# Strided rows loaded as two halves with a gap between them

## The chip, the cores and the metric

The kernel runs on one core of one Trainium2 chip. The metric is the device time of one execution in microseconds (us): lower is better. Before the change, four runs gave a median of 444.38 us (443.89 to 444.83).

## What is computed

Inputs are `q`, `k`, `v` of shape (8, 8, 576, 64) in float32 (batch, heads, positions, head width) and the weights `moe_w_r`, `moe_w_i` (64 modes of 512x512) and `moe_w_ch` (512x512). Half of the heads use a local mask, the other half a strided one:

```
mask_local   = (rel >= 0) & (rel < 32)
mask_strided = (rel >= 0) & (pos[None, :] % 32 == pos[:, None] % 32)
attn = softmax(where(mask, q @ k.T / 8, -1e9)) @ v        # per batch element and head
x    = attn, heads side by side                            # (8, 576, 512)
X    = rfft(x, axis=1)[:, :64]                             # 64 modes
Y    = X times (w_r[m] + i w_i[m]) per mode                # a 512x512 complex matrix each
u    = x + irfft(Y)
out  = u + relu(u @ w_ch)
```

Heads 4 to 7 are the strided ones: a query at position s sees the keys at s, s-32, s-64 and so on. The weights of the 64 modes are 64 x 512 x 512 x 2 float32 numbers, by far the largest part of what is read.

## The kernel before, in words

All large loads are issued by GpSimd (POOL) on one queue, because they convert float32 in memory to float16 on the chip as they are moved. The queue has eight completion semaphores, used in turn: POOL issues a load only when the load eight places before it has landed. Beyond that, a load waits for its target buffer to be free, and since POOL issues in order, everything behind it waits too.

There are three kinds of loads on this queue:

- Strided `q`, `k`, `v` (24 loads, `load(i)` for i below 8, line 200): the four strided heads of one batch element. The 576 positions of a head are 18 blocks (c) of 32 positions (r). One row of a load is one (head, block), so there are 4 x 18 = 72 rows, on 72 partitions. A row is 32 positions x 64 numbers: 8 KB in memory, 4 KB on the chip.
- Local `q`, `k`, `v` (24 loads, line 205): the four local heads, cut into 128 rows of 18 positions x 64 numbers (4.6 KB in memory, 2.3 KB on the chip).
- Weights (254 loads, `w_fetch`, line 180): half of one mode's matrix, 64 rows of 8 KB in memory, 4 KB on the chip. Each mode takes two loads (real and imaginary part on either half of the partitions), once for the first half of the channels and once for the second; mode 0 has no imaginary part. One load of `w_ch` (line 188, 512 packets) is the only other one.

The tile `qn` (pool `pin`, three buffers) holds the three loads of one `load(i)`: `qn[:, 0]` is q, `qn[:, 1]` is k, `qn[:, 2]` is v, each with 2048 columns. v is loaded first, then q, then k.

The work runs in four stages:

1. Strided attention, b = 0 to 7. For each b TensorE transposes the columns of `qn`, 128 at a time (two positions of all 72 rows), into PSUM: `str_q` (line 237, 16 transposes), and `str_turn` for k and v (line 253, 16 each). VectorE and ScalarE copy the results out; then come masks and scores (lines 313 and 321), exponentials (line 328), values (line 342), normalising (lines 217 and 218) and a small Fourier transform `dft` (line 482). The transposes for b+1 stand between the steps of b. At the start of step b POOL gets `load(b + 3)` and a few weight loads: 18 weight buffers are filled in this stage without waiting for one to be used.
2. Local attention, b = 0 to 7, with the modes of the first half between its steps (line 515, 16 matmuls each). From here on each mode that is done frees a weight buffer and has the next fetched.
3. The modes of the second half, with the output's projections between them.
4. Inverse transform, relu, sums and stores.

`load(8)` (the local rows of b = 0) is issued at step b = 5 of stage 1; its first user is the local transpose of line 363.

Of the kernel before, what the change touches and what calls it, by code (L numbers as in the profile page):

```python
# [11 lines left out]
F16 = mybir.dt.float16  # L12
# [65 lines left out]
def kernel(  # L78
# [27 lines left out]
    def psum(kind, half=False):  # L106
        if half:
            return pss[kind].tile([128, 1024], F16, tag=kind, name=kind)
        return pss[kind].tile([128, 512], FP, tag=kind, name=kind)
# [37 lines left out]
    pin = actx.enter_context(tc.tile_pool(name="pin", bufs=3))  # L147
# [41 lines left out]
        w_chs["n"] = w_ch  # L189


    qns = {}

    def load(i):
        if i >= 2 * B:
            return
        qn = pin.tile([128, 3, 2048], F16, tag="qn", name="qn")
        for vi, src in ((2, v), (0, q), (1, k)):
            if i < B:
                nc.gpsimd.dma_start(  # L200
                    qn[0:72, vi, :],
                    src[i, 4:8].rearrange("h (c r) d -> (h c) (r d)", r=32),
                )
            else:
                nc.gpsimd.dma_start(
                    qn[:, vi, 0:1152],
                    src[i - B, 0:4].rearrange("h (cb i) d -> (h cb) (i d)", i=18),
                )
        qns[i] = qn
# [23 lines left out]
    def str_q(b, g):  # L233
        qn, qT = qns[b], qTs[b % 2]
        tp = psum("tp", half=True)
        for i in range(8):
            nc.tensor.transpose(
                tp[:, ds(72 * i, 72)],
                qn[0:72, 0, ds(128 * (8 * g + i), 128)],
                idn[0:72, 0:72],  # L240
            )
        nc.vector.tensor_copy(
            out=qT.rearrange("p (h r c) -> p r h c", h=4, r=16)[:, ds(8 * g, 8)],
            in_=tp[:, 0:576].rearrange("p (r h c) -> p r h c", h=4, c=NCB),
        )

    def str_turn(b, vi, j):
        qn = qns[b]
        a, z = JG[j]
        nr = z - a  # L250
        tp = psum("tp", half=True)
        for i in range(nr):
            nc.tensor.transpose(  # L253
                tp[:, ds(72 * i, 72)],
                qn[0:72, vi, ds(128 * (a + i), 128)],
                idn[0:72, 0:72],
            )

        def move(eng, dst, pr):
            eng(  # L260
                out=dst[:, ds(72 * a, 72 * nr)].rearrange(
                    "p (h c r) -> p h c r", h=4, r=nr
                ),
                in_=tp[pr, 0 : 72 * nr].rearrange("p (r h c) -> p h c r", h=4, c=NCB),
            )

        if vi == 2:
            move(act_copy if j else nc.vector.tensor_copy, vT[:, 0:1152], ds(0, 128))
            return
        for rp in range(2):  # L270
            pr = ds(64 * rp, 64)
            move(
                act_copy if j == 1 else nc.vector.tensor_copy,
                kzs[b % 2][pr, rp, 0:1152],
                pr,
            )

    def str_k(b, j):
        str_turn(b, 1, j)

    def str_v(b, j):
        str_turn(b, 2, j)
# [392 lines left out]

    psum_pools(tp=3, sc=3, av=2)
    load(0)
    const_load(nc.scalar, "cI", "cM6", "cM5", "cFs")
    load(1)
    const_load(nc.sync, "cMl", "cFl", "cA")  # L680
    load(2)
    w_fetch(2)

    def str_front(b):
        return [
            lambda: str_v(b, 0), lambda: str_v(b, 1),
            lambda: str_v(b, 2), lambda: str_q(b, 0),
            lambda: str_back(b, 0),
            lambda: str_back(b, 1), lambda: str_q(b, 1),
            lambda: str_k(b, 0),  # L690
            lambda: str_k(b, 1), lambda: str_k(b, 2),
        ]
# [271 lines left out]
```

The softmax here doesn't subtract the row's maximum and nothing guards it: scores larger than these inputs give would overflow.

## Time and profile before

| what | value |
|---|---|
| median of four runs | 444.38 us |
| the profiled execution | 444.58 us |
| its span in the trace | 442.7 us |
| stage 1 in the trace | about 6 to 82 us |
| POOL's queue of loads | 26608 packets, 81.28 MB as written on the chip |
| read from memory | 163.37 MB |
| TensorE busy | 339.0 us (77%) |
| VectorE, ScalarE busy | 215.7 us (49%), 188.4 us (43%) |
| one issue of a strided load on POOL | 0.53 us |
| issue to landing, strided loads, median | 11.0 us |

The profiled execution's time is 1.9 us above its span: launch and end lie outside. In the page, the span is cut into 40 slices of 11.07 us; a digit is the busy share in tenths. The chain of waits follows the work that ended last back to the start; a piece "DMA qn<-in_q_dram" in it means that the next step waited for this load to land, counted from its issue. The share of the DMA engines in a stretch can be above 1, because the packets that the trace records for one engine overlap a little.

The trace also has a record of every packet: its queue, start, duration and bytes as written. In the steady stage (250 to 360 us) an 8 KB weight row is recorded with 324 ns, and on one engine the next row starts 305 ns after it. The landing of a load is recorded as 16 increments of its semaphore.

### The profile page before, as it was taken

Reading aid. Unit: us, or ns where it says so; the run is one execution under the profiler, and the core shown is the slowest. Engines: PE = TensorE matmul, PEld = TensorE weight load, DVE = VectorE, ACT = ScalarE, POOL = GpSimd, SP = SyncE. Lnnn points to the kernel's source line nnn. Section 1 sums busy time; section 2 is a strip of 40 time slices with the busy share of each in tenths; the row PEclk is TensorE's granted clock in tenths of the full one; section 3 lists DMA queues with packets and bytes.
Section 4 is the critical chain, followed back from the end, with each engine's and each line's share of the span. In section 5 each row is a group of like instructions: output and inputs, shape, how many; then the busy total and the mean of one; then the engine's idle time right before and its main releaser. Section 6 shows DMA issues by size and latency. Waiting matters only on the chain.

```text
span 442.7 us, 12290 instructions
## 1 busy us (share of the span) xinstructions
PE 339.0 (77%) x5284; PEld 242.3 (55%) x5284; DVE 215.7 (49%) x462; ACT 188.4 (43%) x353; POOL 180.6 (41%) x327
## 2 busy tenths in 40 slices
PE   3887789769999886776775458688686849988994
PEld 2766677648777675564653245455444535654441
DVE  3687868744535434151511024345344542763895
ACT  2586667553545554343441302114222402443882
POOL 5243333422544433443443434444444344420883
PEclk9998989675958988675985558588878767998998
DMA  8999999999999999999999999999999999991687
GB/s 186 181 203 201 200 198 203 208 212 206 172 211 212 212 212 211 214 210 213 211 212 212 210 212 213 213 211 211 213 207 211 212 212 212 212 208 30 262 321 273
DMA packets 30902, 92.35 MB, mean 209 GB/s; under 512 B 5952, under 2 KB 6848, under 8 KB 30848
## 3 DMA queue, kind: packets, MB, share of 16 engines
q0 software_dynamic: 26608, 81.28, 93.9%
q1 hardware_dynamic: 3440, 9.50, 5.7%
q8 instruction: 42, 0.69, 0.6%
q10 hardware_dynamic: 800, 0.77, 0.6%
q14 instruction: 12, 0.10, 0.1%
HBM read 163.37 MB, written 9.44 MB: 390 GB/s over the span
## 4 chain that ended last, share of the span: by engine, by line
DMA 65%; PE 25%; DVE 3%; issue 3%; ACT 1%; POOL 1%; DVEq 0%; POOLq 0%; ACTq 0%
DMA wt<-in_moe_w_i_dram 38%; DMA wt<-in_moe_w_r_dram 11%; DMA qn<-in_q_dram 8%; DMA qn<-in_k_dram 5%; PE y L515 4%; PE tp L363 2%; DMA qn<-in_v_dram 2%; PE sc L613 2%; PE v L860 2%; PE v L648 2%; PE u L663 2%; PE sc L409 2%; PE sc L425 1%; PE sc L482 1%; PE y L482 1%
## 5 line engine op out<-in xcount | busy, mean ns | idle before, releaser
L515 PE MATMUL y<-X,wt 128*128 128x16 f16 (+1 forms) x2048 | 82.6, 192 | 62.5 <-DMA wt<-in_moe_w_i_dram 59.6
L180 POOL DMA_DIRECT2D wt<-in_moe_w_r_dram x128 | 66.2, 517 | 133.8 <-DMA wt<-in_moe_w_r_dram 32.4
L515 PEld LDWEIGHTS <-wt 128*128 128x128 f16 (+1 forms) x2048 | 72.1, 103 | 76.0 <-issue 56.2
L180 POOL DMA_DIRECT2D wt<-in_moe_w_i_dram x126 | 65.1, 517 | 61.0 <-DMA wt<-in_moe_w_i_dram 37.6
L622 ACT ACTIVATE v<-sc 128x512 f16<-128x512 f32 x32 | 19.0, 597 | 88.6 <-PE sc L613 88.4
L613 PE MATMUL sc<-w_cp,xT 128*128 128x512 f16 (+1 forms) x160 | 51.2, 449 | 0.5 <-DVE xT L585 0.4
L439 ACT ACTIVATE PL<-sc 128x480 f16<-128x480 f32 (+1 forms) x48 | 27.4, 579 | 37.8 <-PE sc L425 37.4
L623 DVE COPY xo<-tp 128x512 f16<-128x512 f16 x32 | 22.1, 691 | 39.6 <-PE tp L621 39.6
L218 DVE TENSOR_TENSOR xb<-av,rec 90x256 f16<-90x256 f32 (+2 forms) x80 | 36.0, 450 | 2.8
L217 DVE RECIPROCAL rec<-av 90x4 f32<-90x4 f32 (+2 forms) x80 | 14.7, 183 | 46.5 <-PE av L454 32.6
L370 DVE COPY qT<-tp 128x576 f16<-128x576 f16 x16 | 12.0, 758 | 41.1 <-PE tp L363 36.5
L228 ACT ACTIVATE v<-tp 128x640 f16<-128x640 f16 (+1 forms) x24 | 19.4, 808 | 28.0 <-PE tp L397 24.4
L363 PE MATMUL tp<-cI_s,qn 64*64 64x64 f16 x864 | 26.0, 210 | 3.3 <-DMA qn<-in_q_dram 1.8
L328 ACT ACTIVATE PS<-sc 90x360 f16<-90x360 f32 (+1 forms) x48 | 22.8, 489 | 10.3 <-PE sc L321 9.9
L873 POOL TENSOR_TENSOR rl<-rl,xo 128x512 f32<-128x512 f32 x16 | 18.3, 1155 | 18.9 <-ACT rl L871 18.5
L890 DVE TENSOR_TENSOR osb<-u,rl 128x512 f32<-128x512 f32 x36 | 23.8, 689 | 2.7 <-ACT rl L871 1.3
L363 PEld LDWEIGHTS <-qn 64*64 64x64 f16 x864 | 20.4, 122 | 8.2 <-issue 3.0
L482 PEld LDWEIGHTS <-xb 108*128 108x128 f16 (+2 forms) x176 | 18.1, 119 | 12.0 <-DVE xb L218 6.2
L565 DVE COPY xT<-tp 128x512 f16<-128x512 f16 x16 | 11.0, 689 | 25.2 <-DMA wt<-in_moe_w_i_dram 15.6
L409 PE MATMUL sc<-cMl_s,cI_s 128*128 128x480 f16 (+1 forms) x48 | 21.6, 451 | 1.6 <-ACT X L228 1.6
L613 PEld LDWEIGHTS <-xT 128*128 128x128 f16 (+1 forms) x160 | 14.8, 110 | 14.6 <-issue 6.6
L253 PE MATMUL tp<-cI_s,qn 72*128 72x72 f16 x256 | 14.8, 207 | 10.0 <-DMA qn<-in_v_dram 7.2
(94 smaller groups left out, 654.5 us busy)
## 6 DMA issues: line engine op xcount, KB each, us to landing
wt<-in_moe_w_r_dram POOLq DMA_DIRECT2D x128, 256.0 KB, 9.4
wt<-in_moe_w_i_dram POOLq DMA_DIRECT2D x126, 256.0 KB, 9.6
out_dram<-osb SPq DMA_DIRECT2D x14, 512.0 KB, 2.7
qn<-in_v_dram POOLq DMA_DIRECT2D x16, 288.0 KB, 10.5
qn<-in_q_dram POOLq DMA_DIRECT2D x16, 288.0 KB, 10.7
qn<-in_k_dram POOLq DMA_DIRECT2D x16, 288.0 KB, 11.1
out_dram<-osb SPq DMA_DIRECT2D x7, 128.0 KB, 2.4
out_dram<-osb SPq DMA_DIRECT2D x3, 256.0 KB, 2.8
```

Of the source, the lines that this page charges most:

```text
L180: nc.gpsimd.dma_start(wt[ds(64 * ri, 64)], src[m, ds(256 * half, 256), :].rearrange("(p c) e -> p c e", c=4),)
L218: nc.vector.tensor_tensor(out=dst, in0=val.rearrange("p h (q c) -> p h c q", c=4), in1=rec[0:n, 0:pieces] .to_broadcast((n, pieces, 64)) . ...
L228: nc.scalar.activation(out=out, in_=in_, func=ACTF.Copy)
L328: nc.scalar.activation(out=PS[0:n, ds(POFF[t], 4 * n)], in_=scp[0:n, 0 : 4 * n], func=ACTF.Exp, scale=SCALE,)
L363: nc.tensor.transpose(tp[ds(64 * hp, 64), ds(64 * i, 64)], qn[ds(64 * hp, 64), vi, ds(64 * (9 * g + i), 64)], idn[ds(64 * hp, 64), ds(64 * ...
L409: nc.tensor.matmul(scp[:, 0 : n * times].rearrange("p (h x) -> p h x", h=times), idn, mask_rows("cMl", n, times), start=True, stop=False,)
L439: nc.scalar.activation(out=dst, in_=src, func=ACTF.Exp, scale=SCALE)
L482: nc.tensor.matmul(xp[:, ds(192 * cp, 192)], xb[b][0:n, base + t, ds(128 * cp, 128)], F[0:n, t, :], start=(i == 0), stop=(i == len(tiles) ...
L515: nc.tensor.matmul(yv[:, mi, e, :], wt[pr, XC[c], ds(128 * e, 128)], Xh[half][pr, c, :, :, m], start=(c == 0), stop=(c == 3),)
L613: nc.tensor.matmul(vp[pr, :], xT[:, ch, cols], w_chs["cp"][:, ch, :], start=(ch == 0), stop=(ch == 3),)
L623: nc.vector.tensor_copy(out=xo[pr].rearrange("p (h q c) -> p h q c", h=2, c=4), in_=tp[pr, 0:512].rearrange("p (h c q) -> p h q c", h=2, c=4),
L890: nc.vector.tensor_tensor(out=osb[:, t % 2, :], in0=up, in1=rls[b, t][:, t % 2, :], op=AluOp.add)
```

## The change

Each of q, k and v in `qn` gets 2 x 1040 columns instead of 2048: the first half of a row (positions r = 0 to 15 of the block) goes to columns 0 to 1023, the second half (r = 16 to 31) to columns 1040 to 2063, with 16 unused columns behind each half. The target of a strided load is thereby no longer one run of 4 KB per row but two runs of 2 KB, which cannot be merged. The source is the same run of memory, described as 144 runs of 4 KB. The transposes take their 128 columns from the new places (`pair_cols`). The local loads still fill 1152 columns from column 0 of each third, which now starts at multiples of 2080 columns. The order of all instructions on all engines is the same as before.

```
+    HALF = 1024 + 16
     qns = {}
+
+    def pair_cols(i):
+        return ds(HALF * (i // 8) + 128 * (i % 8), 128)
...
-        qn = pin.tile([128, 3, 2048], F16, tag="qn", name="qn")
+        qn = pin.tile([128, 3, 2 * HALF], F16, tag="qn", name="qn")
         for vi, src in ((2, v), (0, q), (1, k)):
             if i < B:
                 nc.gpsimd.dma_start(
-                    qn[0:72, vi, :],
-                    src[i, 4:8].rearrange("h (c r) d -> (h c) (r d)", r=32),
+                    qn[0:72, vi, :].rearrange("p (f x) -> p f x", f=2)[:, :, 0:1024],
+                    src[i, 4:8].rearrange("h (c f r) d -> (h c) f (r d)", f=2, r=16),
                 )
...
-                qn[0:72, 0, ds(128 * (8 * g + i), 128)],
+                qn[0:72, 0, pair_cols(8 * g + i)],
...
-                qn[0:72, vi, ds(128 * (a + i), 128)],
+                qn[0:72, vi, pair_cols(a + i)],
```

## The prediction, made before the result was known

> **What bounds the kernel now.** I read the page's slices first, then the DMA queues, the chain of waits, the issues on POOL's queue and last TensorE's waits. From the page:
>
> ```profile
> span 442.7 us, 12290 instructions
> ...
> DMA  8999999999999999999999999999999999991687
> GB/s 186 181 203 201 200 198 203 208 212 206 172 211 212 212 212 211 214 210 213 211 212 212 210 212 213 213 211 211 213 207 211 212 212 212 212 208 30 262 321 273
> ...
> q0 software_dynamic: 26608, 81.28, 93.9%
> ...
> DMA 65%; PE 25%; DVE 3%; issue 3%; ACT 1%; POOL 1%; DVEq 0%; POOLq 0%; ACTq 0%
> ```
>
> The DMA engines are full until the last tenth, and the chain is 65% DMA. From slice 11 on, where only weights and local rows are loaded, the rate stays at 210 to 214 GB/s; in slices 2 to 6, where the strided rows are loaded, it is 198 to 203, equally full by the digits. The packet count tells why. The known packets of POOL's queue are 254 x 64 weight rows, 24 x 128 local rows, 24 x 72 strided rows, 512 for w_ch and 16 completion writes for each of 303 loads: 26416. The 192 left are 8 per strided load, and 72 + 8 = 80 = 16 x 5: the 72 rows are dealt five to an engine and filled up. So 14 engines move five rows, one two, one none. The landings say the same: of the 16 increments of the first v load two come at 4.02 and 4.99 us, the other fourteen between 5.62 and 6.33; of the load at 63.88 us two come at 65.48 and 66.79, fourteen between 72.96 and 74.97. A load is as late as its busiest engine, and the engines' queues are never empty.
>
> The chain of waits in 0 to 100 us:
>
> ```profile
> 5.03 14.49 DMA qn<-in_q_dram
> 19.52 0.28 issue
> 19.80 11.64 DMA wt<-in_moe_w_r_dram
> 31.44 0.28 issue
> 31.73 11.39 DMA qn<-in_k_dram
> 43.11 0.28 issue
> 43.40 10.53 DMA qn<-in_q_dram
> ...
> 71.36 10.66 DMA qn<-in_q_dram
> 82.02 0.04 issue
> 82.07 1.17 PE tp L363 x19
> ```
>
> Each piece is one turn of the eight semaphores: a load lands, the load eight later is issued. The local stage starts at 82.07 because the first local q landed at 82.02; all 24 strided loads are ahead of it on the queue. From 82 to 148 us the chain runs through TensorE, and from 148.6 to 373 through weight loads, eight per 9.91 us (1.239 us each). The stream of weights is full again from about 121 us; a delay or gain at 82 us goes through to the end. How much TensorE waited in stage 1 (timeline of TensorE; in brackets idle before):
>
> ```profile
> 52.35 0.53 PE L253 MATMUL tp<-cI_s,qn 72*128 72x72 f16 x11 [0.82 <-DMA qn<-in_v_dram]
> 53.98 0.62 PE L237 MATMUL tp<-cI_s,qn 72*128 72x72 f16 x8 [0.43 <-DMA qn<-in_q_dram]
> ```
>
> After the first load it waits for no rows until 52.35 us, then 0.8, 0.4, 0.5 (q near 64), 0.3 (q near 73) and 1.8 us (before 82.07): 3.8 in all. So the loads are only just the slower side: TensorE can use up to 3.8 us.
>
> **The change, part by part.** The sum stands against the profiled execution, 444.58 us (span 442.7 plus 1.9 around it); the median is 0.20 lower.
>
> *Price of a packet.* In the trace's packet records the distance between two packets of one engine is 304.7 ns for 8192 bytes read, 172.7 for 4608, 78.8 for 2048, and about 18.5 for a completion write (4 x 304.7 + 18.5 = 1237, against 1239 paced). First and last give 0.03677 ns per byte and 3.5 ns per packet (4608 bytes: 172.9). A half row of 4096 bytes, an estimate between rows: 154.1 ns. Splitting 1728 rows thus costs 1728 x 3.5 / 16 = 0.4 us in all.
>
> *Dealing the pieces.* Before, the busiest engine spends 5 x 304.7 + 18.5 = 1542 ns on a strided load. If the 144 pieces come out even, nine to an engine, it is 9 x 154.1 + 18.5 = 1405. That is 137 ns for each of 24 loads, **-3.3 us**, the 0.4 already in it. The pace of POOL's issues bounds it from above: three strided and four weight loads take 60.27 - 50.28 = 9.99 us and then 69.93 - 60.27 = 9.66, less 4 x 1.239 is 1.57 to 1.68 per strided load, so -4.0 to -6.6, which TensorE's 3.8 cuts off. From below: pieces grouped by row, ten on 14 engines, 1541 + 18.5 = 1560, **+0.4 us**; or twelve engines, the most that share 72 rows evenly, with 12 pieces each, 1868 ns: even in the long run if the twelve move on from load to load, **+7.8 us** if they are always the same. [...]
>
> [...]
>
> *Issues on POOL.* w_ch with 512 packets held POOL 782 ns, a weight load with 64 rows 515: 0.6 ns per packet, 0.05 us for 72 more, 1.1 us over 24 loads. It hides behind POOL's wait for a semaphore (0.8 to 1.8 us before the strided issues above); only the first issue has no cover, **+0.05 us**. Without cover it would be the 1.1.
>
> *Transposes and buffer.* The 384 transposes read the same 128 adjacent columns at another place: 95 to 99 ns per load into TensorE before, 102 to 110 for those of the local rows. Ends 0 and 384 x 10 ns = 3.8 us; I take 0, since the shape stays and the loads overlap the matmuls (192 ns). The 192 bytes more per partition in each third of `qn` issue nothing. The local rows start elsewhere, with the same 128 runs: 0.
>
> No wait is added and no step moved; POOL's first gated issues, v of each load, wait for TensorE to free `qn`, and move with it.
>
> Sum: 444.58 - 2.8 + 0.05 = 441.8, so **441.6** beside the median. Late next at 82 us would be TensorE itself.
>
> **The rivals.**
>
> *By rows after all (nothing gained).* The pieces of one partition stay on one engine: 24 x 17.5 ns = 0.4 us more, **444.8**. [...]
>
> *The same few engines (slower).* One mechanism: strided loads no longer reach all 16 engines, and always leave out the same ones. Place: every strided load. Price 326 ns x 24 = 7.8 us, **452**. It decides once the busiest engine averages more than 9.9 pieces a load ((1542 - 18.5) / 154.1). For it: 72 and 144 have no common share on 16; against: before used 15.
>
> *Dearer pieces.* The second half starts 2080 bytes into a row of the tile, and no row shows 2 KB writes there. At nine to an engine the gain is gone at 169 ns per piece; at 174 it is +1.0 us, **445.4**.
>
> *TensorE takes it back.* The loads get earlier, but stage 1 keeps its pace (TensorE busy 8.5 of 10 us in 60 to 70): only some 1.3 us remain, **443.1**.
>
> **How the numbers follow.** A measurement here tells about 0.2% (0.9 us) from no change. Forecast 0.54, its own range 440.4 (all of the 3.8) to 442.5; TensorE takes it back 0.08; by rows 0.16; the same few engines 0.12; dearer pieces 0.10. Faster 0.54 + 0.08 = 0.62, within 0.2% 0.16, slower 0.22. The range goes up to 445.4 and leaves out the few engines and about half of the dearer pieces.
>
> **What would show it.** The queue has 28144 packets if each of 24 x 72 rows becomes two (+1728) and the 192 fillers go (-192); with fillers for rows, 28528. Strided GB/s rise from 201 to about 207; the fourteen-and-two in the landings disappears; the load before line 363 lands near 79 instead of 82.02, with TensorE's waits for rows in stage 1 nearly gone; the 1.239 us of the weight stream stay. Wrong: packets of 2 KB recorded far apart from 154 ns, landings in groups of twelve and four that never move, or 82.02 unchanged with earlier landings.

## The result and the profile after

Over 40 runs the changed kernel takes a median of 445.41 us (443.19 to 448.59) beside 443.89 us over 61 runs of the kernel before. The ratio is 1.0039 [1.0028, 1.0051]: slower by 0.4%, some 1.7 us. Forecast were 441.6 us and a range of 440.4 to 445.4: the direction is wrong, and the time lies at the upper end, just outside. Here and below, medians are over all runs, and ratios leave out the few runs that were over 1.5% above the fastest of their kernel. The profiled execution took 447.52 us, its span is 445.7 us (before 442.7).

The page of the changed kernel, the lines that answer to those shown of before:

```profile
span 445.7 us, 12290 instructions
...
DMA  8999999999799999999999999999999999991687
GB/s 167 168 195 200 204 200 202 211 212 210 145 212 212 211 213 210 212 211 214 212 211 209 212 212 212 212 212 213 211 209 209 211 211 212 213 211 36 260 319 271
...
q0 software_dynamic: 29296, 81.29, 95.4%
...
DMA 68%; PE 22%; issue 4%; DVE 3%; ACT 1%; POOL 0%; DVEq 0%; POOLq 0%
```

Three things are to be seen. The rate in the first two slices fell from 186 and 181 GB/s to 167 and 168, and in the next five it stayed where it was (195 to 204). The packets' share of the engines' time on POOL's queue rose from 93.9% to 95.4% for the same bytes, from 415.7 to 425.2 us by the two spans; of these 9.5 us some 2.4 are only the way packets are recorded (two halves of 173 ns for a row of 324), the rest is mostly longer packets. And there are 29296 packets. Before there were 26608; 1728 halves more make 28336, and 960 are left, 40 for each strided load on top of the 8 fillers of before. 48 fillers are 4 engines x 12: a load of 144 pieces goes to twelve engines, twelve pieces each, and the four others are filled up. The landings of single loads show four early increments and twelve later ones (the first v: 4.41 to 5.62 us, then 6.27 to 10.03), and no engine is far ahead any more (the last strided load: all sixteen between 73.41 and 77.22 us; before, two of its sixteen came at 65.48 and 66.79 and the others from 72.96 on). So the twelve move on from load to load.

The chain of waits of the changed kernel (start, length in us, what):

```profile
1.34 0.87 POOL qn L207
2.21 10.32 DMA qn<-in_q_dram
12.58 0.66 PE tp L244 x8
...
18.23 11.55 DMA qn<-in_v_dram
29.78 0.28 issue
30.06 10.67 DMA wt<-in_moe_w_i_dram
...
63.87 11.06 DMA qn<-in_v_dram
74.93 0.28 issue
75.22 9.37 DMA qn<-in_q_dram
84.63 1.17 PE tp L370 x36
```

It has the same form as before: turns of the eight semaphores, and at the end the local q, which lands at 84.59 us (before 82.02). These 2.6 us are most of the 2.9 us between the two profiled executions (447.52 and 444.58): what comes late there goes through to the end, as the prediction had it. TensorE's waits between 6 and 90 us (engine, line, what it waited for: us in total, times, longest):

```profile
PE tp L260 <- DMA qn<-in_v_dram: 12.7, 4, 10.1
...
PE tp L370 <- DMA qn<-in_q_dram: 2.0, 1, 2.0
PE tp L244 <- DMA qn<-in_q_dram: 1.6, 2, 1.4
```

and the same of before:

```profile
PE tp L253 <- DMA qn<-in_v_dram: 7.2, 2, 6.4
...
PE tp L363 <- DMA qn<-in_q_dram: 1.8, 1, 1.8
```

Line 260 is line 253 of before, and line 370 line 363: the first v landed at 10.03 us instead of 6.33. The timeline of POOL at the start shows a part of that:

```profile
1.34 0.87 POOL L207 DMA_DIRECT2D qn<-in_v_dram  x1 [0.90 <-POOLq L955]
2.21 0.71 POOL L207 DMA_DIRECT2D qn<-in_q_dram  x1
2.92 0.69 POOL L207 DMA_DIRECT2D qn<-in_k_dram  x1
...
10.32 0.69 POOL L207 DMA_DIRECT2D qn<-in_k_dram  x1 [3.31 <-DMA qn<-in_v_dram]
```

An issue takes 0.69 us where it took 0.53. The first packet of a strided load starts at 3.84 us instead of 3.18.

In the packet records, 62% of the pieces of 2 KB (as written) are recorded with 172 to 173 ns, at a distance of 154 ns from the next one on their engine, as forecast. The others are longer, 6% of all 300 ns and more. Their mean by stretch: 219 ns in 0 to 6 us, 239 in 10 to 20, 195 in 20 to 30, 184 to 189 from 30 to 90. So 62% of the packets, called undisturbed below, cost what the prediction said, and more than a third cost more.

To put a price on it, take the time from the landing of the 24th load to the landing of the local q: it holds 18 weight loads, two local loads and nine strided ones. It is 38.91 us before and 39.58 after. Less 25.1 us for 18 weight loads (1.239 each) and two local ones (8 x 172.7 + 18.5 ns each), that is 1.54 and 1.61 us for a strided load. The forecast was 1.405.

### The profile page after: what moved, and what is told of

Read it like the earlier page. It is cut to its first block, busy times and chain, and to the rows that moved or that the text cites. A ratio compares the mean times of both kernels' runs of the same rounds, so it can differ in the third digit from the quotient of the medians.

```text
span 445.7 us, 12290 instructions
## 1 busy us (share of the span) xinstructions
PE 342.1 (77%) x5284; PEld 245.3 (55%) x5284; DVE 215.9 (48%) x462; ACT 188.3 (42%) x353; POOL 184.9 (41%) x327
## 3 DMA queue, kind: packets, MB, share of 16 engines
q0 software_dynamic: 29296, 81.29, 95.4%
## 4 chain that ended last, share of the span: by engine, by line
DMA 68%; PE 22%; issue 4%; DVE 3%; ACT 1%; POOL 0%; DVEq 0%; POOLq 0%
DMA wt<-in_moe_w_i_dram 47%; DMA wt<-in_moe_w_r_dram 9%; DMA qn<-in_v_dram 5%; DMA qn<-in_q_dram 4%; PE y L522 4%; PE sc L620 2%; DMA qn<-in_k_dram 2%; PE tp L370 2%; PE v L867 2%; PE v L655 2%; PE u L670 2%; PE sc L416 1%; PE sc L432 1%; PE u L886 1%; DVE yy L649 1%
## 5 line engine op out<-in xcount | busy, mean ns | idle before, releaser
L522 PEld LDWEIGHTS <-wt 128*128 128x128 f16 (+1 forms) x2048 | 73.0, 104 | 72.9 <-issue 46.8
L377 DVE COPY qT<-tp 128x576 f16<-128x576 f16 x16 | 12.1, 758 | 42.7 <-PE tp L370 38.1
L370 PE MATMUL tp<-cI_s,qn 64*64 64x64 f16 x864 | 26.9, 214 | 3.6 <-DMA qn<-in_q_dram 2.0
L489 PEld LDWEIGHTS <-xb 108*128 108x128 f16 (+2 forms) x176 | 17.6, 117 | 11.8 <-DVE xb L225 5.8
L416 PE MATMUL sc<-cMl_s,cI_s 128*128 128x480 f16 (+1 forms) x48 | 22.5, 468 | 1.6 <-ACT X L235 1.6
L432 PE MATMUL sc<-qT,kz 128*128 128x160 f16 (+1 forms) x160 | 22.7, 269 | 0.0
```

Of the source, the lines that this page charges most:

```text
L370: nc.tensor.transpose(tp[ds(64 * hp, 64), ds(64 * i, 64)], qn[ds(64 * hp, 64), vi, ds(64 * (9 * g + i), 64)], idn[ds(64 * hp, 64), ds(64 * ...
L416: nc.tensor.matmul(scp[:, 0 : n * times].rearrange("p (h x) -> p h x", h=times), idn, mask_rows("cMl", n, times), start=True, stop=False,)
L432: nc.tensor.matmul(scp[:, ds(col, n)], kzs[par][:, hp, ds(s0, 128)], qTs[par][:, ds(s0, n)], start=False, stop=(i == len(todo) - 1),)
L522: nc.tensor.matmul(yv[:, mi, e, :], wt[pr, XC[c], ds(128 * e, 128)], Xh[half][pr, c, :, :, m], start=(c == 0), stop=(c == 3),)
```

## The experiments

**Where does the loss arise, and is it the odd start?** Three theories stood at first. A: the loss is made at the start, by the first loads; B: every split load is dearer; C: the second half, 2080 bytes into a row of the tile, is written slowly (the rival "dearer pieces"). The first four kernels ran on one chip with one set of runs of the kernel before.

The loads of b = 0 to 2 whole, the others as halves:

```
+    def halves(b):
+        return b >= 3
...
+                if halves(i):
                     ... the two halves ...
+                else:
+                    nc.gpsimd.dma_start(qn[0:72, vi, 0:2048], ...)
```

> The strided rows of batch elements 0 to 2 (nine loads) are loaded whole, as before the change; those of 3 to 7 (fifteen loads) stay in halves. Theory A (the loss is made at the start, where nine split loads stand back to back and TensorE waits for the first of them until 10 us instead of 6.4): the first load lands at about 6.3 us again and the kernel is no slower than before, 443 to 444 us, or faster by up to 15 x 0.137 = 2 us if the later halves do come cheaper. Theory B (pieces are dear wherever they stand, about 1.6 us a load in the later part of stage 1 against 1.54 whole): 15 x 0.07 = 1 us slower than before, about 445.

Measured: 445.31 us beside 445.2, ratio 0.9995 [0.9976, 1.0015]. The reverse, only the loads of b = 0 to 2 as halves (`return b < 3`):

> The reverse: only the nine loads of batch elements 0 to 2 are in halves, the other fifteen whole. Theory A: the whole loss stays, first landing at about 10 us, 445 to 446 us. Theory B: 9 x 0.07 us, 444.5 at most.

Measured: 445.4 us, ratio 0.9992 [0.9975, 1.001]. Neither part alone shows a loss that can be told from nothing: B's 1 us (a ratio of 1.002) lies outside the first interval, A's 1 to 2 us outside the second. The change itself was not run on this chip, so that its loss is smaller there is not excluded. The traces say more: with the first three split the first v landed at 7.56 us, and the ninth load at 20.60, earlier than before (21.97). A falls, as a loss that the first loads always bring. With the later loads split the stretch from the 24th load to the local q takes 40.53 us, so 1.71 us for a strided load; with them whole again 39.13 us, 1.56. That has B's sign, in one execution each.

The gap between the halves 128 columns instead of 16:

```
-    HALF = 1024 + 16
+    HALF = 1024 + 128
```

> The change with a gap of 128 columns instead of 16, so that every half row starts at a multiple of 256 bytes of its partition. Theory C (the pieces are dear because the second half starts at an odd multiple of 32 bytes): the pieces' median and upper quarter come down to 173 ns, the first landing of a strided load comes back from 10.0 to below 7 us, and the kernel gains the forecast 2 to 3 us, 441 to 442. Theories A and B: nothing changes, 445 to 446.

Measured: 445.1 us, ratio 0.9999 [0.9984, 1.0014]. The pieces still have a mean of 187 to 202 ns, and a strided load costs 1.56 us. The odd start is not what makes the pieces dear. What is left of it, 0.05 us a load against the 1.61 of the change, is no more than single executions differ by: a second one of the changed kernel, below, also takes 1.56. But since this ratio and the first one of the change do not overlap, a share for the gap is not excluded either.

**The loads alone.** A kernel that holds only phases of 24 loads, nine buffers, nothing else on the queue:

```
+    phase("sa", [128, 2080], split(72, 1040))    # as the change
+    phase("sb", [128, 2304], split(72, 1152))    # gap of 128
+    phase("wc", [128, 2048], whole(64))
+    phase("sc", [128, 2080], split(64, 1040))
+    phase("wd", [128, 2048], whole(128))
+    phase("we", [128, 4096], pair)               # 72 rows x 2 batch elements, whole
+    phase("sd", [128, 2080], split(128, 1040))
```

> Nothing but loads: eight groups of 24 back to back on POOL, all else of the kernel left out and zeros stored. Pace per load from the later issues. wa, 72 whole rows: 1.54 us as in the kernel. sa, 72 rows in halves with a gap of 16 columns: 1.40 if the pieces come even and cost 154 ns, 1.6 or more if they are dear by themselves, 1.87 if the same twelve engines always do them. sb, the same with a gap of 128 columns: as sa, or 1.40 if the odd start was the price. wc, 64 whole rows: 1.24. sc, 64 rows in halves: 1.25 at 154 ns a piece; clearly above if halves are dear without any uneven split. wd, 128 whole rows: 2.46. sd, 128 rows in halves: 2.48. we, 72 rows of two batch elements in one load (144 whole rows, two runs per partition, so the split over engines is that of the halves): 3.66 x 12/16 = 2.8 us if twelve engines move on and rows cost 304.7 ns; more if that split itself is the price.

Us per load from the landing of the 8th load of a phase to that of the 24th, and the mean recorded duration of a packet:

| phase | pieces | us per load | at even dealing | packet, ns |
|---|---|---|---|---|
| sa | 72 rows in halves, gap 16 | 1.546 | 1.405 | 208 |
| sb | 72 rows in halves, gap 128 | 1.509 | 1.405 | 200 |
| wc | 64 whole rows | 1.243 | 1.237 | 330 |
| sc | 64 rows in halves | 1.273 | 1.251 | 183 |
| wd | 128 whole rows | 2.458 | 2.456 | 327 |
| sd | 128 rows in halves, gap 16 | 2.486 | 2.484 | 175 |
| we | 144 whole rows on 72 partitions | 3.150 | 2.76 | 402 |

The third column comes from the prediction's packet prices (sd: 16 x 154.1 + 18.5 ns). The phase of 72 whole rows ran beside the stores of zeros and is not used; it was run again below. The windows of sa, we and sd (stretch, length, VectorE and POOL busy, granted clock, share of the DMA engines, GB/s):

```profile
70.00:106.00 36.00, 0.00 (x0) 13.44 (x25) 1.00 1.22 183
...
290.00:362.00 72.00, 0.00 (x0) 11.92 (x22) 1.00 1.15 184
370.00:425.00 55.00, 0.00 (x0) 13.64 (x24) 1.00 1.12 211
```

Halves with the small gap on 128 partitions cost what was forecast, to 2 ns a load, at 211 GB/s. Whole rows without any halves, 144 of them on 72 partitions, cost 14% more than even dealing and run at 184 GB/s. By the packet count they also go to twelve engines: the run has 3648 packets beyond rows, halves and completion writes, 152 for each of 24 loads over the eight phases, which is 8 for the 72 whole rows and 48 each for sa, sb and we. So C falls, and halves as such fall too: what is dear goes with 72 partitions dealt to twelve engines.

**Reading or writing side?** It is assumed here that each of the twelve engines takes a run of neighbours, six rows of the tile and so twelve halves; the trace does not name the engine of a packet. The theories now: R, the reading side (which parts of memory twelve engines read at once); P, the place on the chip to which they write. The same loads to partitions 0 to 71 and to partitions 32 to 103 read the same memory:

```
-            t[0:n, :]
+            t[base : base + n, :]        # n = 72, base 0 or 32
```

> Nothing but loads again, eight groups of 24 (all else of the kernel left out, zeros stored at the end): each form of the 72 rows once on partitions 0 to 71 and once on 32 to 103. wa and wf: 72 whole rows; sb and sf: halves, gap 128; sa and sg: halves, gap 16; we and wg: rows of two batch elements in one load. Theory P (twelve engines that write runs of six neighbouring partitions meet at the same places of the on-chip memory, and 64 of the 72 rows lie in the first 64 partitions): on 32 to 103 the meeting is rarer, sf and sg fall from 1.5 to 1.6 us towards 1.40, wg from 3.1 towards 2.76, while wa and wf stay at 1.54, set by the engine with five rows. Theory R (the price is on the side of reading, twelve streams 48 KB apart): no difference between the two places.

The total is from the first issue to the last landing.

| load | us per load at 0 | at 32 | total of 24 at 0 | at 32 | packet at 0, ns | at 32 |
|---|---|---|---|---|---|---|
| 72 whole rows (wa, wf) | 1.538 | 1.531 | 40.22 | 40.70 | 332 | 336 |
| halves, gap 128 (sb, sf) | 1.556 | 1.394 | 42.72 | 38.67 | 212 | 178 |
| halves, gap 16 (sa, sg) | 1.511 | 1.403 | 41.81 | 38.80 | 202 | 177 |
| 144 whole rows (we, wg) | 3.181 | 2.763 | 82.38 | 73.56 | 409 | 333 |

The windows of sb, sf, sa, sg, we, wg in this order (stretch, length, POOL busy, granted clock, share of the DMA engines, GB/s):

```profile
100.00:120.00 20.00, 7.41 (x13) 1.00 1.26 182
140.00:160.00 20.00, 8.29 (x15) 1.00 1.13 208
182.00:202.00 20.00, 7.40 (x13) 1.00 1.24 188
224.00:242.00 18.00, 6.72 (x12) 1.00 1.13 208
270.00:325.00 55.00, 8.46 (x16) 1.00 1.16 181
350.00:400.00 50.00, 9.33 (x18) 1.00 1.07 211
```

With everything equal but the place, the rate goes from 181 to 188 GB/s to 208 to 211, and the share of the DMA engines is 1.07 to 1.13 instead of 1.16 to 1.26. On partitions 32 to 103 a split load costs 1.39 to 1.40 us: the forecast of 1.405, with twelve engines here too (7296 fillers in this run, 304 per load over its phases: 2 x 8 and 6 x 48). So for loads on twelve engines the place on the chip is shown to set the price, as P has it, and R falls. In the kernel, whose transposes read the rows from partition 0 on, the other place wasn't tried.

The totals show more than the pace. At 0 the split loads keep the pace of whole rows (1.51 to 1.56 against 1.538), so their forecast gain is gone; but all 24 take 41.8 to 42.7 us (42.4 and 41.8 in the run before this one) against 40.2. The difference of 1.6 to 2.5 us, the size of the kernel's loss, is made for the most part by the first eight loads, which POOL issues without a wait: the eighth lands 17.6 to 17.8 us after the first issue, with whole rows 15.6 (at 32: 16.4 and 16.2).

That pieces meet each other on partitions 0 to 71, and where, was the author's guess; no run shows it. The place alone doesn't make loads dear either: 72 whole rows are as fast at 0 as at 32 (1.538 and 1.531 us), and 64 whole rows at base 0 cost 1.243 us against 1.237 at even dealing: there an engine takes five rows, or four, and not six.

**The change again, and 64 and 8 rows.** The next kernels went to another chip, as the loads at 0 and 32 did, the changed kernel without any edit among them:

> The changed kernel itself once more, beside the kernel before on the same chip, so that the three variants run earlier (all within 0.2% of before) have their counterpart. Theory A+B (the change costs some 1 to 2 us on any chip): ratio 1.002 to 1.005, first strided landing later than 7.5 us. Theory D (the size of the loss belongs to the execution, not to the split): ratio within 0.2% of 1.

Measured: 446.44 us beside 445.37, ratio 1.002 [0.9993, 1.0047]. It agrees with the first result and, by itself, with no change. Its trace shows the same marks: first v at 9.28 us, 167 and 179 GB/s in the first slices, the local q at 84.30 us.

If the forecast's error is the dealing (theory E: what makes the pieces dear is the dealing of 72 rows to twelve engines, and what counts is an even share per engine), then 64 rows, four to an engine, and 8 rows by themselves should bring what was promised: 8 pieces on each of 16 engines, and 16 pieces on eight engines that move on, nine on average.

```
+                for rows in (ds(0, 64), ds(64, 8)):
+                    nc.gpsimd.dma_start(
+                        qn[rows, vi, :].rearrange(...)[:, :, 0:1024],     # HALF = 1024 + 128
+                        src[i, 4:8].rearrange(...)[rows],
+                    )
```

> Each strided load is cut into 64 rows and 8 rows, both in halves with a gap of 128 columns. 64 rows come out at four to each of 16 engines (measured alone, 64 rows in halves: 1.27 to 1.31 us a load, hardly above 64 whole rows), the other 8 on eight engines in turn. Theory E (what makes the pieces dear is the dealing of 72 rows to twelve engines, not the halves): 1.29 + (2 x 0.154 + 0.02) / 2 = 1.45 us per strided load against 1.54, so 2 us faster than before, less what 24 more issues on POOL cost: 442 to 444 beside 445. Theory B (halves are dear wherever they are): no gain, 445 or more.

Measured: 442.22 us beside 445.37 (8 runs, 439.03 to 448.88), ratio 0.992 [0.9887, 0.9954]. The page of this kernel:

```profile
span 438.3 us, 12330 instructions
...
GB/s 187 208 210 211 210 209 210 212 210 213 210 213 210 213 211 212 212 211 213 211 211 213 212 212 211 212 201 210 213 211 213 211 211 213 211 189 33 250 335 260
...
q0 software_dynamic: 28912, 81.29, 94.6%
...
DMA 52%; PE 30%; DVE 8%; issue 5%; ACT 4%; POOL 0%; DVEq 0%; POOLq 0%
```

The strided loads now run at 208 to 211 GB/s, as fast as weights. Of the 28912 packets 384 are fillers, 16 for each strided load: eight idle engines x 2 for the rest of 8 rows, none for the 64. The pieces have a mean of 173 to 178 ns. Between the landings of two weight loads at 56.11 and 65.34 us lie three strided and four weight loads in 9.23 us; less 4 x 1.239 that is 1.425 us for a strided load; nine pieces and two completion writes are 9 x 154.1 + 2 x 18.5 = 1424 ns, and with the rest always on the same engines it would be ten pieces, 1578. The local q lands at 77.41 us instead of 82.02, and stage 1 no longer hangs on loads: the chain is 52% DMA, and between 6 and 90 us TensorE's transposes wait for rows once, at the first v:

```profile
PE tp L263 <- DMA qn<-in_v_dram: 7.9, 1, 7.9
```

To see whether the halves or the cut into 64 and 8 bring it (theory F), the kernel before with the same cut and whole rows:

```
+                for rows in (ds(0, 64), ds(64, 8)):
+                    nc.gpsimd.dma_start(qn[rows, vi, :], src[i, 4:8].rearrange("h (c r) d -> (h c) (r d)", r=32)[rows])
```

> [...] Theory E (the gain of the run with halves is the even share: its busiest engine has 4.5 rows a load): here the busiest has 4 + 1 rows and one completion write more, 5 x 0.305 + 2 x 0.018 = 1.56 us a load, so 0.4 us slower than before or the same, 445 beside 445. Theory F (the gain comes from cutting 64 rows off, which are dealt by place, and not from evenness): as fast as the run with halves, 442.

Measured: 443.35 us beside 444.38, ratio 0.9994 [0.9967, 1.0021]: no change. Its strided slices stay at 197 to 206 GB/s, as before. The 4 + 1 rows of theory E take for granted that the eight rows go to the same engines each time, which no run had shown. The kernel has 8 fillers for each load, as before; a rest that moved on would make 4.5 rows on average, 4.5 x 304.7 + 2 x 18.5 = 1408 ns. Over the same stretch as above, up to the landing of the local q, a strided load takes 1.61 us here, and 1.42 in each of the two executions with halves. So the eight rows are taken to go to the same engines each time, five rows on the busiest as before. By the loads F falls: the cut alone brings nothing, and what it brings with halves is that the rest of 16 pieces moves on. By the times alone F is less clearly out, since this interval and that of the next run overlap a little. The kernel with 64 and 8 rows in halves, a second time, with the same set of runs of the kernel before:

> The run with 64 and 8 rows in halves once more, because its times were spread over 439 to 449. Theory E: a ratio of 0.989 to 0.995 again, 440 to 443 beside 445.

Measured: 441.83 us (440.37 to 447.81) beside 444.38, ratio 0.9953 [0.9925, 0.9981]. Faster again, by 0.5% instead of 0.8%. This version is faster than the kernel before, and than the changed one too: 442.22 against 446.44 us on the one chip where both ran.

The profiled execution of this last run lies near the upper end of its times, span 444.8 us against 438.3, though its local q landed at 77.38 us as in the first. The windows of both (stretch, length, then TensorE, weight loads into it, VectorE, ScalarE, POOL busy, granted clock, DMA share, GB/s) show where the gain went. The first:

```profile
60.00:80.00 20.00, 16.36 (x323) 13.73 (x321) 16.58 (x48) 15.31 (x34) 10.73 (x20) 1.00 1.09 210
...
100.00:110.00 10.00, 9.74 (x231) 8.02 (x230) 3.98 (x10) 6.62 (x13) 4.07 (x8) 1.00 1.07 212
```

and the second:

```profile
60.00:80.00 20.00, 16.95 (x255) 14.50 (x252) 14.59 (x40) 14.02 (x32) 10.62 (x20) 0.83 1.08 210
...
100.00:110.00 10.00, 10.00 (x199) 8.32 (x198) 4.32 (x8) 3.76 (x6) 2.98 (x6) 0.50 0.91 165
```

Most of it goes in stage 1. From 60 to 80 us TensorE got through 255 instructions at a granted clock of 0.83 instead of 323 at 1.00 (from 40 to 60 us 0.78 and 1.00), and it came to the first local transpose at 83.12 us instead of 78.26, although the local q had landed at 77.4 in both. That is 4.9 of the 6.5 us between the spans. The rest is lost behind it: at a clock of 0.50 TensorE is busy without a break, and the loads that wait for its weight buffers run at 165 GB/s instead of 212. The profiled run of 64 and 8 whole rows has the same clock (0.87 over the first 80 us, as the second here; the first has 0.98). Its local q landed only at 80.55 us, but its first local transpose starts at 83.11, and its span is 444.6. In such an execution TensorE, not the loads, sets when stage 1 ends, and rows that come 3.2 us earlier bring nothing. Why the clock was granted so differently no run shows.

## Why the prediction was wrong

**Price of a packet: right.** 154 ns between undisturbed halves, and 2.486 us for a load of 256 of them, 2.484 by the working.

**Dealing the pieces: here it failed.** The step of the sum "if the 144 pieces come out even, nine to an engine" took as its price 9 x 154.1 + 18.5 = 1405 ns. The dealing was named as one of two possible ones: twelve engines with twelve pieces that move on, which is nine on average. What failed is that twelve moving engines were given the price of an even nine. On partitions 0 to 71 pieces dealt so are dearer: a load costs 1.51 to 1.56 us alone and 1.56 to 1.71 in the kernels, instead of 1.405. Against the 1.542 us of before, the term of -3.3 us is by these loads -0.8 to +4.1 (24 x -0.03 to 24 x 0.17); 24 loads alone, with their start, took 1.6 to 2.5 us longer than whole rows. That the same loads at 32 to 103 take 1.39 to 1.40 us, and that 64 and 8 rows take 1.42 in the kernel and make it faster, shows that the rest of the step held. The upper bound from POOL's pace in that step (1.57 to 1.68 us for a whole-row load of before) was too high: 72 whole rows take 1.538 alone, and 1.54 in the kernel before from the 24th load to the local q, which is the 1542 ns of the five rows. The sum takes 2.8 of the 3.3 us; no run shows these 0.5 us. What the runs show in their place is a start that is slower by more (next paragraph).

**First landings: much later than these prices give.** Twelve pieces on an engine instead of five rows, 1868 ns against 1542 by the prediction's prices, would make the first v 0.3 us later. It landed 3.7 us later in the profiled execution, and 1.2 to 3.0 us later in three other kernels whose first loads are split (7.56, 8.20, 9.28). The pieces are dear there (219 ns in 0 to 6 us).

**Issues on POOL: mis-sized.** The 0.6 ns per packet, taken from a load of a different form, gave 0.05 us for an issue; it became 0.16 (0.69 instead of 0.53). Over 24 loads that is 3.8 us rather than 1.1. The cover was named rightly, POOL's wait for its semaphores, and holds for the later strided issues but two (the q at 45.30 and at 64.61 us follow their v without a wait). But it is not only the first issue that has none: the first eight have none, and the eighth starts at 6.33 us instead of 5.03.

**Transposes and buffer: right.** The weight loads of the strided transposes take 95 ns at the least and 99 in the median, as before. (The buffer grows by 64 bytes per partition in each third, 192 in all three, not by 192 in each.)

**The cap of 3.8 us from TensorE's waits: not contradicted, but it belongs to one execution.** 64 and 8 rows landed the local q 4.6 us earlier and brought 3.2 and 2.5 us in the medians; with the clock of the second profiled execution there would have been nothing to gain. (With the cap taken whole the range begins at 440.6, not 440.4.)

**The rivals.** By rows: excluded by the packet count. The same few engines: excluded, they move on (the last strided load of the change has all sixteen increments between 73.41 and 77.22 us). Dearer pieces forecast 445.4 and came closest; its price is right (174 ns a piece makes 1.58 us of a load, and the traces of the changed kernel and of the wider gap give 1.56 to 1.61), and its cause is not: neither the odd start (1.56 us a load with the gap of 128) nor the size of a piece (175 ns in halves on 128 partitions), but the place on the chip and the dealing to twelve engines (202 to 212 ns at partitions 0 to 71, 177 and 178 at 32 to 103). That its time is met so closely is partly luck: it stands for 1.0 us above before, and measured are 1.5 in the medians, some of them made by the first landings and not by nine dearer pieces. TensorE takes it back: not in the change, but seen in one execution of the kernel that does get its rows early.

**What stays open.** How the 1.7 us divide between the start and the later loads: either part alone gave a ratio that can't be told from 1, and so did the gap of 128. The traces lean to the start: in the profiled executions the ninth load of the changed kernel lands 2.35 us late (24.32 against 21.97) and the local q 2.57, and alone the first eight loads make most of it; but with only the first nine split the ninth landed at 20.60. Which engine writes which partitions, and whether and where the pieces meet, no run shows.

## What to carry to other kernels

More and smaller pieces don't balance a load by themselves (144 of them went to twelve engines): work out from the packet count how many engines they are dealt to, and then measure that load by itself at its own partitions. The loads on twelve engines cost 7 to 13% less at another place (1.403 us against 1.511, 2.763 against 3.181), the 72 whole rows the same (1.531 and 1.538). For the 72 rows here, a load of 64 rows and a small one of 8, whose pieces move from engine to engine, were better than one load in finer pieces (442.22 us beside 446.44). And the distance of undisturbed packets gave about the lowest price of a split load that was seen (1.405 us by it, 1.39 to 1.40 at partitions 32 to 103), not its price at 0 to 71 (1.51 to 1.56).

## What was not expected of the hardware

- The place of the target on the chip alone changed the rate of twelve engines from 181 to 211 GB/s (144 whole rows at partitions 0 to 71 and 32 to 103).
- By the packet counts, engines that a load leaves out still get packets: 48 fillers of 4 bytes for a load on twelve engines, 16 for the rest of eight rows in halves.
- Issuing a load of 144 pieces held POOL for 0.69 us, a load of 72 whole rows for 0.52.
- Two executions of one kernel, with the same landings up to 77.4 us, had a granted clock of 1.00 and 0.83 from 60 to 80 us, and 1.00 and 0.50 from 100 to 110; the first local transpose came at 78.26 and 83.12 us, and the spans were 438.3 and 444.8.
